# New transfer allowances and dates for the weight conversions that a planner makes ahead, and narrower ring dependencies

## The chip, the cores and the metric

The kernel runs on one core of one Trainium2 chip. The metric is the device time in microseconds (us) of one execution; less is better. The time of the kernel before is the median of three runs, and one further execution was taken by the hardware profiler.

## The reference, cut to what matters

An attention over 12 blocks of 128 tokens (two batches of 768, eight heads of 64, a local band of 96 tokens and 8 global ones) gives x of 1536 x 512. Two feed-forward layers follow, each 512 to 2048 to 512, all in float32 (the weights are float64 on the host):

```python
x = attention(q, k, v).reshape(1536, 512)
h = np.maximum(x @ moe_w_in, 0.0);  x = (h * h) @ moe_w_out
h = x @ moe2_w_in
g = np.where(h >= 1, h, np.where(h <= -1, 0.0, (h + 1) ** 2 / 4))
out = g @ moe2_w_out
```

## The kernel before

**Precision.** TensorE works on float32r, so each float32 operand is split into a high and a low part, and each product is three matmuls (high-high, low-high, high-low). ScalarE (ACT) makes the high part by a copy and VectorE (DVE) the low part by a subtraction (`copy` and `rest` of `Plan`).

**Weights.** A weight block c (128 hidden units of one layer, both matrices, 128x1024 float32) arrives as float64 words: two loads of 512 KB into a tile of the ring `raw` (two tiles). `float32` makes it float32 in a tile of the ring `whole` (three tiles in the middle of the kernel, two of them for good; the third lies in the tile m): for each half one ACTIVATE on ACT and three passes on DVE. `make` then splits it into one of nine slots from which TensorE reads it.

**Conversions made ahead.** The second layer runs through all its weights twice, and in pairs of blocks, with one product fewer per pair by the scheme of Strassen and Winograd, for which sums of the blocks are needed. So `prepare` converts each pair of blocks (c, c + 1) once, ahead, while the first layer still computes: four loads into `raw`, four ACTIVATEs, twelve DVE passes, two stores of 512 KB to DRAM (`kept`), four subtractions on GpSimd (POOL) or DVE into the tile `sumt`, and a store of that (`sums`). There are eight such preparations. Later `make_kept` loads `kept` and `sums` back into `whole` tiles and splits them into slots.

**Order.** Nothing is issued as it is written: every step is handed to a planner (`Plan.op`, `Plan.any_of`) with the engine or engines that may run it, a duration in ns, a due time and the keys it reads and writes. `emit` then runs a list schedule: an engine that is free takes, of the steps whose dependencies are met, the one that is due first. The order that comes out is the program order on each engine; on the chip the engines wait on semaphores only, so an engine whose next step is not ready stands, with all that is queued behind it. A step's `lag` is added to its end before its dependents may start: transfers have 1456 ns for 512 KB and, so far, `LAG` = 950 ns behind it. The keys also order the rings: a tile's next writer follows the readers of the one before, in the order in which the steps are handed in.

**Due times** count in events, one of which is a block of 128 hidden units against 512 tokens (24 matmuls of 512 columns). The first layer has 52 events (u = 0 to 51) with a total of 48 units; the 16 pair steps follow with 2.816 units each. `run` walks through the events and calls `prepare` for the next pair as soon as an event's due time reaches the preparation's date, which is `PREP + PREP_STEP * n`. With the dates before these are the events 25, 29, 32, 35, 38, 41, 44 and 47. The reloads of the first pair that need a slot of the first layer are handed in after events 45 and 46 (`make_after`).

**Places.** In the pair steps the accumulators p, u2, u3, u4 lie in a ring `u` of eight places of 384 columns in the tile pr; columns 0 to 2047 of pr hold the first layer's results of tokens 1024 to 1535 (keys `("save", 2, k)`) and columns 2048 to 3071 are `sumt`. `Plan.before` gives keys that the first writer of a place must also wait for. The lines that the change touches are the constants at L33, `float32` (L452), `prepare` (L484) and `instead` (L1292).

Of the kernel before, what the change touches and what calls it, by code (L numbers as in the profile page):

```python
# [29 lines left out]
G_LEAD = 2  # L30


PREP, PREP_STEP, LATE = 21, 3.1, 1  # L33
FIRST = -0.6, -0.4, 0.8

WARM, LAG = 10, 950
# [32 lines left out]
class Plan:  # L69
# [27 lines left out]
    def op(self, engine, ns, due, fn, reads=(), writes=(), lag=0, rows=P, tail=False, port=False):  # L97
        self.any_of([(engine, ns, fn, port)], due, reads, writes, lag, rows, tail=tail)
# [204 lines left out]
def ns_dve(n):  # L303
    return n / 0.96 + 70
# [11 lines left out]
class Ffn:  # L316
# [132 lines left out]
        plan.copy(w, d + 0.6, hi, f32[:, o:1024], keys, his, engines=WCOPY)  # L449
        plan.rest(w, d + 0.7, lo, f32[:, o:1024], hi, keys + his, los, engines=WREST)  # L450

    def float32(self, layer, c, due):  # L452

        nc, op = self.nc, self.plan.op
        kc, f32 = self.ring("whole")
        kr, raw = self.ring("raw")
        low, high, word = raw[:, :, 0], raw[:, :, 1], f32.bitcast(U32)
        for n in range(2):
            op("dma", 1456, due - W_LOAD + 0.1 * n, lambda n=n: nc.sync.dma_start(
                out=raw[:, 512 * n:512 * n + 512].rearrange("p f t -> p (f t)"), in_=self.w[layer][n][c],  # L460
            ), (), [(*kr, n)], lag=LAG)
        for n in range(2):
            h = slice(512 * n, 512 * n + 512)
            d = due - W_MAKE + 0.4 * n

            self.plan.scale(512, d, f32[:, h], high[:, h].bitcast(F32), 2.0 ** -112, [(*kr, n)], [(*kc, n)], engines=CONV)
            op("dve", ns_dve(256), d + 0.1, lambda h=h: nc.vector.tensor_scalar(  # L467
                out=word[:, h], in0=word[:, h], scalar1=3, scalar2=None, op0=ALU.logical_shift_left,
            ), (), [(*kc, n)], port=True)
            op("dve", ns_dve(512), d + 0.2, lambda h=h: nc.vector.scalar_tensor_tensor(  # L470
                out=word[:, h], in0=low[:, h], scalar=29, in1=word[:, h],
                op0=ALU.logical_shift_right, op1=ALU.bitwise_or,
            ), [(*kr, n)], [(*kc, n)], port=True)
            op("dve", ns_dve(512), d + 0.3, lambda h=h: nc.vector.scalar_tensor_tensor(  # L474
                out=word[:, h], in0=high[:, h], scalar=0x80000000, in1=word[:, h],
                op0=ALU.bitwise_and, op1=ALU.bitwise_or,
            ), [(*kr, n)], [(*kc, n)], port=True)
        return kc, f32
# [5 lines left out]
    def prepare(self, c, due):  # L484

        nc, op, plan = self.nc, self.plan.op, self.plan
        keys, tiles = [], []
        for n in range(2):
            kc, f32 = self.float32(1, c + n, due + LATE + n)
            ks = [(*kc, h) for h in range(2)]  # L490
            op("dma", 1456, due + LATE + 1 + n, lambda n=n, f32=f32: nc.sync.dma_start(out=self.kept[c + n], in_=f32),
               ks, [("kept", c + n)], lag=LAG)
            keys.append((*kc, 0))
            tiles.append(f32)
        kt, t = self.ring("sumt")
        SUMS = [("dve", ns_dve, nc.vector), ("pool", ns_pool, nc.gpsimd)]
        b11, b21, b12, b22 = (f32[:, 256 * n:256 * n + 256] for f32 in tiles for n in range(2))
        t1, t2, t3, t4 = (t[:, 256 * n:256 * n + 256] for n in range(4))
        for n, (out, in0, in1) in enumerate(((t1, b12, b11), (t3, b22, b12), (t2, b22, t1), (t4, b21, t2))):
            plan.any_of([(way, ns(256), lambda en=en, out=out, in0=in0, in1=in1: en.tensor_tensor(  # L500
                out=out, in0=in0, in1=in1, op=ALU.subtract), True) for way, ns, en in SUMS],
                due + LATE + 1 + 0.1 * n, keys, [kt])
        op("dma", 1456, due + LATE + 2, lambda: nc.sync.dma_start(out=self.kept_sums[c // 2], in_=t),
           [kt], [("sums", c)], lag=LAG)

    def parts(self, i, due, kc, f32):
        plan = self.plan
# [676 lines left out]
def kernel(  # L1184
# [38 lines left out]
    kept = [[dram.tile([P, 1024], F32, name=f"{name}{c}") for c in range(n)] for name, n in (("kept", 16), ("sums", 8))]  # L1223

    def tiles(s, f, plan):
# [18 lines left out]
        save = [pool.tile([P, 2048], F32, name=f"save{i}") for i in range(2)]  # L1244
# [47 lines left out]
        def instead():  # L1292

            b = f.plan.before
            for i in range(8):
                b["u", i] = [("save", 2, k) for k in range(4)] + [("sumt", 0)]
            for i in range(4):
                for part in range(2):
                    b["gq", i, part] = [("g512", i, part)] if i < 2 else [
                        (a, N_SLOTS - 1, h) for a in ("hi", "lo") for h in range(2)]  # L1300
            for i in range(2):
                b["rq", i] = [("r512", i)]
                for part in range(2):
                    b["xs", 4 + i, part] = [("raw", i, h) for h in range(2)]
                    b["o", 1 + i, part] = [("save", 3, k) for k in range(4)]
# [127 lines left out]
```

## Time and profile before

| what | value |
|---|---|
| median of 3 runs | 625.58 us |
| the three runs | 621.22, 625.58, 628.64 us |
| profiled execution | 628.68 us, of which the span from first to last instruction is 626.7 us |
| granted TensorE clock, mean | 0.99 |
| busy share of PE, DVE, ACT, POOL | 97%, 78%, 56%, 9% |
| bytes moved | 78.71 MB, mean 126 GB/s |

The profiled execution is 0.5% above the median and as long as the longest of the three runs. A busy share is the part of the span in which the engine had an instruction running; the two us between time and span lie outside the instructions.

### The profile page before, as it was taken

The page shows a single profiled execution, that of the slowest core. Times are in us where ns is not written, and L with a number is a line of the kernel's source. Part 1 is how long each engine was busy: PE and PEld are TensorE (multiplying, and loading weights), DVE is VectorE, ACT ScalarE, POOL GpSimd, SP SyncE. Part 2 cuts the span into 40 slices and gives each one's busy share as a digit, 9 for nine tenths or more (in the row PEclk, how much of TensorE's full clock was granted, in tenths as well). Part 3 has the DMA queues.
Part 4 walks back from the last instruction along what each step waited for, and adds up shares of the span by engine and source line. Part 5 has one row for each costly group of instructions (what it writes and reads, how often), then busy time and mean ns, then how long its engine had stood idle before and what let it go on. Part 6 is the DMA issues. An engine that isn't in the chain of part 4 may idle for free. (4 is left out here: it accounts for less than half of the span.)

```text
span 626.7 us, 9687 instructions
## 1 busy us (share of the span) xinstructions
PE 605.8 (97%) x3439; PEld 516.5 (82%) x3439; DVE 486.4 (78%) x1056; ACT 348.6 (56%) x720; POOL 58.5 (9%) x86
## 2 busy tenths in 40 slices
PE   7999999999999999979999999999999999999995
PEld 4788987887888888758888878888899888899884
DVE  5899999985638997768438569999988678887862
ACT  3898776965547765445347455554544445454431
POOL 4122020120100202222200200000000000000000
PEclk8999999999999999989999999999999999999999
DMA  7445444440014776896610430222220032222002
GB/s 268 150 150 173 135 153 135 136 169 18 27 41 133 252 258 237 274 352 236 210 55 0 155 132 35 93 93 94 93 92 35 0 136 93 92 93 92 27 1 106
DMA packets 25689, 78.71 MB, mean 126 GB/s; under 512 B 3104, under 2 KB 3104, under 8 KB 25632
## 3 DMA queue, kind: packets, MB, share of 16 engines
q1 hardware_dynamic: 25344, 78.00, 36.0%
q8 instruction: 29, 0.48, 0.3%
q14 instruction: 28, 0.23, 0.1%
q10 hardware_dynamic: 288, 0.00, 0.0%
HBM read 62.26 MB, written 15.73 MB: 124 GB/s over the span
## 5 line engine op out<-in xcount | busy, mean ns | idle before, releaser
L137 DVE TENSOR_TENSOR g<-r,g 128x512 fp32r<-128x512 f32 (+2 forms) x74 | 47.8, 646 | 36.0 <-ACT g L126 35.1
L655 DVE TENSOR_TENSOR pr<-bank,pr 128x384 f32<-128x384 f32 x112 | 60.0, 553 | 18.6 <-PE bank L649 17.7
L547 ACT ACTIVATE r<-bank 128x512 f32<-128x512 f32 (+1 forms) x52 | 29.2, 562 | 53.4 <-PE bank L532 52.1
L126 ACT ACTIVATE g<-r 128x512 fp32r<-128x512 f32 (+2 forms) x74 | 42.7, 577 | 23.3 <-DVE r L564 14.3
L893 ACT ACTIVATE pr<-pr,mn 128x256 f32<-128x256 f32 (+1 forms) x96 | 45.9, 482 | 10.3 <-DVE mn L888 10.0
L150 ACT ACTIVATE whole<-raw 128x512 f32<-128x512 f32 x52 | 34.0, 670 | 24.4 <-DMA raw<-in_moe_w_in_dram 7.7
L560 ACT ACTIVATE r<-pr,small 128x384 f32<-128x384 f32 x43 | 26.3, 616 | 33.8 <-DVE pr L655 33.6
L154 POOL TENSOR_SCALAR pr<-pr,mn 128x256 f32<-128x256 f32 (+1 forms) x39 | 25.4, 661 | 129.9 <-DVE mn L900 52.8
L474 DVE SCALAR_TENSOR_TENSOR whole<-raw,whole 128x512 uint32<-128x512 uint32 x52 | 37.3, 724 | 0.3
L470 DVE SCALAR_TENSOR_TENSOR whole<-raw,whole 128x512 uint32<-128x512 uint32 x52 | 36.9, 720 | 0.5
L888 DVE CUSTOM_DVE_ANT_0 pr<-bank,m 128x256 f32<-128x256 f32 (+1 forms) x96 | 33.2, 394 | 5.0 <-PE bank L952 5.0
L865 PEld LDWEIGHTS bank<-nat,nat 64*128 64x128 f32 x352 | 24.4, 200 | 9.9 <-issue 3.0
L467 DVE TENSOR_SCALAR whole<-whole 128x512 uint32<-128x512 uint32 x52 | 24.0, 468 | 10.6 <-ACT whole L150 9.8
L865 PE MATMUL bank<-nat,nat 64*128 64x128 f32 x352 | 28.9, 299 | 3.3 <-DVE mn L888 2.4
L562 DVE SCALAR_TENSOR_TENSOR r<-r 128x384 f32<-128x384 f32 x43 | 23.8, 556 | 6.0 <-ACT r L560 5.3
L126 ACT ACTIVATE pr<-bank 128x512 f32<-128x512 f32 (+2 forms) x47 | 24.3, 523 | 5.8 <-PE bank L916 2.3
L560 ACT ACTIVATE nat<-pr,small 128x384 f32<-128x384 f32 x21 | 12.9, 617 | 24.3 <-DVE pr L655 24.3
L564 DVE TENSOR_TENSOR r<-pr,r 128x384 f32<-128x384 f32 x43 | 23.8, 557 | 1.2
L916 PE MATMUL bank<-ident,pr 128*128 128x128 f32 x176 | 24.3, 277 | 0.2 <-DVE pr L152 0.2
L952 PE MATMUL bank<-pr,nat 128*64 128x128 f32 x352 | 23.6, 277 | 0.2
L916 PEld LDWEIGHTS bank<-ident,pr 128*128 128x128 f32 x176 | 20.3, 142 | 3.6 <-issue 0.9
L952 PEld LDWEIGHTS bank<-pr,nat 128*64 128x64 f32 x352 | 19.4, 136 | 4.2 <-issue 2.0
(343 smaller groups left out, 1755.6 us busy)
## 6 DMA issues: line engine op xcount, KB each, us to landing
raw<-in_moe_w_in_dram SPq DMA_DIRECT2D x32, 512.0 KB, 4.1
raw<-in_moe_w_out_dram SPq DMA_DIRECT2D x32, 512.0 KB, 4.1
whole<-sums SPq DMA_DIRECT2D x14, 512.0 KB, 3.2
whole<-kept SPq DMA_DIRECT2D x13, 512.0 KB, 3.2
kept<-whole SPq DMA_DIRECT2D x12, 512.0 KB, 6.2
whole<-kept SPq DMA_DIRECT2D x13, 384.0 KB, 2.9
sums<-pr SPq DMA_DIRECT2D x8, 512.0 KB, 6.0
nat<-in_k_dram SPq DMA_DIRECT2D x12, 256.0 KB, 3.5
```

Of the source, the lines that this page charges most:

```text
L126: ("act", ns_act(n) - 30 * psum, lambda: nc.scalar.activation(out=at(out), in_=in_, func=ACTF.Copy), False),
L137: ways = [("dve", ns_dve(n), lambda: nc.vector.tensor_tensor(out=at(out), in0=in_, in1=at(hi).bitcast(F32), op=ALU.subtract), not psum)]
L150: ("act", ns_act(n) + (0 if isinstance(by, float) else 107), lambda: nc.scalar.activation(out=out, in_=in_, func=ACTF.Copy, scale=by), False),
L470: op("dve", ns_dve(512), d + 0.2, lambda h=h: nc.vector.scalar_tensor_tensor(out=word[:, h], in0=low[:, h], scalar=29, in1=word[:, h], op0 ...
L474: op("dve", ns_dve(512), d + 0.3, lambda h=h: nc.vector.scalar_tensor_tensor(out=word[:, h], in0=high[:, h], scalar=0x80000000, in1=word[: ...
L560: op("act", ns_act(N) + 64, due, lambda: nc.scalar.activation(out=r, in_=h, func=ACTF.Relu, bias=self.half, scale=0.5), keys, [kr])
L655: op("dve", ns_dve(W), start + step[name] + 0.2 - G_LEAD, lambda: nc.vector.tensor_tensor(out=to, in0=area[kb], in1=in1, op=ALU.add), [("b ...
L865: nc.tensor.matmul(**c)
L888: op("dve", ns_dve(w), due, lambda e=e: nc.vector.tensor_tensor_reduce(out=pr[:, e, :w], in0=self.banks[kbs[e % 2]][:, e // 2 * 256:e // 2 ...
L893: op("act", ns_act(w) + 200, due, lambda e=e: nc.scalar.activation(out=pr[:, e, :w], in_=pr[:, e, :w], func=ACTF.Exp, bias=mn[:, e:e + 1], ...
L916: self.nc.tensor.transpose(self.banks[kbs[m]][:, o:o + P], pr[:, 2 * m + e, c * P:(c + 1) * P], self.ident)
L952: nc.tensor.matmul(**c)
```

## The change

The constants that date the preparations are changed: the first at 20 units in place of 21, and one every 2.75 units in place of 3.1. With these the calls fall to the events 24, 27, 30, 33, 35, 38, 41 and 44. A new constant `SLOW` = 3500 ns takes the place of `LAG` = 950 ns behind the transfers of a preparation (its loads of raw words, its stores to `kept`, its store to `sums`), so the planner lets a dependent start 4956 ns after such a transfer starts, where it was 2406 ns (and the hand-over between engines on top in both). The loads of `make` and `make_kept` keep `LAG`. In `instead`, a place of the ring `u` no longer waits for all of `save` 2 and `sumt`: places 0 to 5 wait for `save` 2, places 5 to 7 for `sumt`, as the columns lie. No instruction is added or taken away.

```diff
-PREP, PREP_STEP, LATE = 21, 3.1, 1
+PREP, PREP_STEP, LATE = 20, 2.75, 1
+
+SLOW = 3500
...
-    def float32(self, layer, c, due):
+    def float32(self, layer, c, due, lag=LAG):
...
                 out=raw[:, 512 * n:512 * n + 512].rearrange("p f t -> p (f t)"), in_=self.w[layer][n][c],
-            ), (), [(*kr, n)], lag=LAG)
+            ), (), [(*kr, n)], lag=lag)
...
-            kc, f32 = self.float32(1, c + n, due + LATE + n)
+            kc, f32 = self.float32(1, c + n, due + LATE + n, SLOW)
             ks = [(*kc, h) for h in range(2)]
             op("dma", 1456, due + LATE + 1 + n, lambda n=n, f32=f32: nc.sync.dma_start(out=self.kept[c + n], in_=f32),
-               ks, [("kept", c + n)], lag=LAG)
+               ks, [("kept", c + n)], lag=SLOW)
...
         op("dma", 1456, due + LATE + 2, lambda: nc.sync.dma_start(out=self.kept_sums[c // 2], in_=t),
-           [kt], [("sums", c)], lag=LAG)
+           [kt], [("sums", c)], lag=SLOW)
...
             for i in range(8):
-                b["u", i] = [("save", 2, k) for k in range(4)] + [("sumt", 0)]
+                b["u", i] = [("save", 2, k) for k in range(4)] * (i < 6) + [("sumt", 0)] * (i > 4)
```

## Rows read from the trace of the kernel before

**Rows 1.** The page, part 1: busy us, share and instructions of each engine

```profile
PE 605.8 (97%) x3439; PEld 516.5 (82%) x3439; DVE 486.4 (78%) x1056; ACT 348.6 (56%) x720; POOL 58.5 (9%) x86
```

**Rows 2.** Waits of engine PE: line, releaser, us in total, times, longest

```profile
...
PE bank L532 <- ACT r L547: 4.5, 1, 4.5
...
PE bank L730 <- DVE g L137: 1.4, 1, 1.4
PE bank L649 <- ACT pr L126: 1.3, 1, 1.3
...
```

**Rows 3.** Windows: stretch, length, busy of each engine, clock, DMA share, GB/s

```profile
...
270.65:275.15 4.50, 0.00 (x1) 0.00 (x0) 3.05 (x6) 1.16 (x3) 2.47 (x3) 1.00 0.97 347
275.15:282.00 6.85, 6.85 (x23) 5.47 (x24) 4.97 (x9) 4.52 (x9) 0.80 (x2) 0.75 0.92 319
...
363.00:615.00 252.00, 252.00 (x1250) 226.38 (x1249) 209.17 (x370) 118.92 (x198) 0.00 (x0) 1.00 0.21 73
...
```

**Rows 4.** Timeline of ACT, 240 to 280: start, length, work, [idle before, releaser]

```profile
...
245.35 0.67 ACT L150 ACTIVATE whole<-raw 128x512 f32<-128x512 f32 x1 [4.35 <-DMA raw<-in_moe_w_out_dram]
...
257.33 1.23 ACT L150 ACTIVATE whole<-raw 128x512 f32<-128x512 f32 x2 [5.25 <-DMA kept<-whole]
...
269.11 1.23 ACT L150 ACTIVATE m<-raw 128x512 f32<-128x512 f32 x2 [4.77 <-DMA kept<-m]
273.95 0.66 ACT L150 ACTIVATE whole<-raw 128x512 f32<-128x512 f32 x1 [3.62 <-DMA raw<-in_moe_w_in_dram]
...
```

**Rows 5.** Timeline of all engines where PE stood still

```profile
...
262.61 0.74 PE L730 MATMUL bank<-g,slot4h 128*128 128x512 f32 x2 [1.45 <-DVE g L137]
...
275.15 0.50 PE L532 MATMUL bank<-x,slot6h 128*128 128x512 f32 x1 [4.50 <-ACT r L547]
...
361.31 1.06 ACT L126 ACTIVATE slot3h<-whole 128x1024 fp32r<-128x1024 f32 x1 [2.44 <-DMA whole<-sums]
362.28 0.47 ACT L126 ACTIVATE pr<-bank 128x384 f32<-128x384 f32 x1
...
362.80 0.44 PE L649 MATMUL bank<-xs,slot0h 128*128 128x384 f32 x1 [1.26 <-ACT pr L126]
...
```

**Rows 6.** DMA issues, whole span: count, KB each, median us to landing

```profile
raw<-in_moe_w_in_dram SPq DMA_DIRECT2D x32, 512.0 KB, 4.1
...
kept<-whole SPq DMA_DIRECT2D x12, 512.0 KB, 6.2
...
```

**Rows 7.** The same from 262 to 275 us alone

```profile
...
kept<-whole SPq DMA_DIRECT2D x2, 512.0 KB, 8.3
...
```

**Rows 8.** Line L491 (stores of kept), 340 to 356 us: landing times

```profile
DMA to landing us min/median/max: 2.6/3.0/3.4
```

**Rows 9.** Timeline of SP's queue: stores of the sums, last step of each preparation

```profile
...
264.93 0.32 SPq L503 DMA_DIRECT2D sums<-pr  x1
...
276.06 0.33 SPq L503 DMA_DIRECT2D sums<-pr  x1
...
311.69 0.42 SPq L503 DMA_DIRECT2D sums<-pr  x1
...
355.47 0.43 SPq L503 DMA_DIRECT2D sums<-pr  x1
```

**Rows 10.** Windows of 10 us, columns as in the other windows

```profile
...
210.00:220.00 10.00, 10.00 (x46) 8.29 (x45) 9.62 (x16) 7.70 (x13) 1.45 (x2) 1.00 0.86 296
...
310.00:320.00 10.00, 10.00 (x46) 8.28 (x45) 0.82 (x2) 3.73 (x6) 0.00 (x0) 1.00 0.47 155
...
```

**Rows 11.** The page, part 5: ACT's and DVE's passes of one conversion

```profile
L150 ACT ACTIVATE whole<-raw 128x512 f32<-128x512 f32 x52 | 34.0, 670 | 24.4 <-DMA raw<-in_moe_w_in_dram 7.7
...
L474 DVE SCALAR_TENSOR_TENSOR whole<-raw,whole 128x512 uint32<-128x512 uint32 x52 | 37.3, 724 | 0.3
L470 DVE SCALAR_TENSOR_TENSOR whole<-raw,whole 128x512 uint32<-128x512 uint32 x52 | 36.9, 720 | 0.5
...
L467 DVE TENSOR_SCALAR whole<-whole 128x512 uint32<-128x512 uint32 x52 | 24.0, 468 | 10.6 <-ACT whole L150 9.8
```

## The prediction

> **What bounds the kernel.** I read the page's first part before anything else: PE is busy 605.8 of 626.7 us [rows 1], so the sum of the matmuls sets the time, and nothing that another engine does counts unless PE stands. The list of PE's waits tells where it stands. It has ten entries, of which seven, 6.3 us together, lie in the first 60 us, long before any step that the change dates. The other three are all that PE loses after that [rows 2]. From 363 to 615 us, the pair steps, PE is busy without a gap [rows 3]. So the change can only work between about 200 and 363 us, where the preparations run, and what it can win there is those three stops.
>
> The timeline says what they are [rows 5]. At 262.61 PE had stood 1.45 us for the low part of g on DVE; at 275.15 it had stood 4.50 us for a bank that ACT had not emptied; at 362.80 it had stood 1.26 us for ACT's copy of the first pair product. Behind each stands ACT in its own order of work, waiting for a transfer. Before the first, ACT waited 5.25 us at 257.33 for a store of `kept` that still read the `whole` tile that the next conversion was to fill; before the second, 4.77 us at 269.11 for another such store, and then 3.62 us at 273.95 for raw words [rows 4]; before the third, 2.44 us at 361.31 for a reload of sums, with the copy queued behind it [rows 5]. The same view has a wait of 4.35 us at 245.35 that cost PE nothing [rows 4]. So PE bears somewhat over 4 us of a late ACT, and pays from there on.
>
> The 4.50 us have a second price. In the 6.85 us after them the granted clock was 0.75 of full speed [rows 3], that is part at 2.4 and part at 1.2 GHz: a quarter of 6.85 us, 1.71 us, is lost. Together the stops cost 1.45 + 4.50 + 1.71 + 1.26 = 8.92 us of the profiled execution.
>
> Why ACT stood is an error of the planner. It placed the dependents of a transfer 1456 + 950 = 2406 ns after its start. Stores of `kept` took 6.2 us in the median and loads of raw words 4.1 [rows 6], and around the two large stops the stores took 8.3 [rows 7], while the DMA engines were 97% busy at 347 GB/s [rows 3].
>
> **The change part by part.** *The allowance of 3500 ns.* It changes no instruction, only which one ACT and DVE take next and when a tile's next use is planned. A dependent is now placed 4956 ns after the transfer's start. That is above the raw loads' 4.1 us and 1.24 us short of the stores' 6.2. An ACT that arrives 1.24 us early is far inside the 4 us that PE bears. But at 8.3 us it would be 3.34 us early, and two such waits in a row would pass the mark again. So it matters whether the transfers stay as crowded.
>
> I think that they don't. A preparation moves seven transfers of 512 KB, 3.67 MB. The last stores of the fourth and the fifth lie 276.06 - 264.93 = 11.13 us apart [rows 9], which is 330 GB/s, the rate at which the DMA engines were full. The planner packed them so closely because it thought the tiles free 2.55 us too early. Each conversion now holds its raw tile 2.55 us longer in the plan. With two such tiles that is 1.28 us per conversion, 2.55 us per preparation: about 13.7 us for one, my estimate from these rows, or 268 GB/s, three quarters of what ran at 97%. Stores then come nearer to the 2.6 to 3.4 us of a quiet stretch [rows 8] than to 8.3. I take nothing for the stops at 262 and 275 us and the clock after them, a gain of 1.45 + 4.50 + 1.71 = 7.66 us; the other end, if crowding stays, is no gain.
>
> *The dates.* A full event has 24 matmuls, and 46 matmuls fill 10 us [rows 10], so a unit is about 5.2 us. The first preparation is asked for 5.2 us earlier, and the step falls from 16.2 to 14.3 us. That calls the eighth at event 44 in place of 47. This is more than a date. Before, two reloads for the first pair had been handed in after events 45 and 46, ahead of it; they held both `whole` tiles until slots of the first layer came free. So the seventh preparation's sums were stored at 311.69 and the eighth's at 355.47, 43.8 us apart [rows 9]. Now it stands ahead of the reloads. Counting 13.7 us each from the fourth (264.93, less the 5.2 us of the earlier date) the eighth ends near 315 us. What moves is all of it: four loads and three stores on SP's queue, four ACTIVATEs of 670 ns (2.7 us), twelve DVE passes, 4 x (724 + 720 + 468) ns = 7.6 us [rows 11], and four subtractions on POOL. They enter a stretch in which DVE worked 0.82 us of 10 and ACT 3.73 [rows 10], so I cost them at nothing there; if that cover is gone, they cost no more than the 1.26 us that they cost at their old place. They leave the 15 us before the first pair, where they delayed the slot copies and reloads that ACT stood for at 361.31. On SP's queue the eighth is moved past the first reloads, which then go out some 20 us later; they are needed shortly before 362.80 [rows 5], which leaves over 20 us.
>
> On the other side the second and third preparations enter a stretch in which DVE was 96% busy, 210 to 220 us [rows 10]. The 7.6 us of a preparation don't fit into such a stretch. The bounds are nothing, because steps for PE are due earlier and go first, and 1.45 us, the nearest row in which a late low part of g stopped PE [rows 5]. I take nothing, for DVE at 96% let PE run through [rows 10], and keep 1.45 for the range.
>
> *The ring `u`.* The first write of place 0, the copy at 362.28 [rows 5], had to follow the last store of sums in the plan, issued at 355.47 [rows 9]. Without that key it may come earlier; with the eighth preparation gone by 315 us the key would not bind either. Together the two edits are worth between 0 and the 1.26 us of that stop. I take 1.26, since what ACT waited for there goes away with the eighth preparation. Places 6 and 7 belong to the second pair and meet nothing. No wait is added on the chip by any of this: the semaphores follow the tiles, and these stay.
>
> **The sum.** 628.68 - 8.92 = 619.76 us if every stop goes. A new order rarely closes without a small gap; I leave half of the smallest stop, 0.65 us, and forecast 620.4 us. The median of 625.58 lies 3.1 us below the profiled execution and the shortest run, 621.22, only 1.5 us above the floor, so I take the stops to differ from run to run with the landing times, and the gain against the median is 5.2 us, 0.8%.
>
> **The rivals.** *The transfers stay crowded, so the change doesn't do what it says.* If the planner fills the freed time with reloads and the loads of `make`, stores take 8.3 us again and the stops stay: 625.6 us, the median. For it: 4956 ns is well under 8.3. Against it: the longer hold of the tiles itself thins the traffic. A milder form keeps one stop of 4.50 with its 1.71 us of clock and loses the rest, 619.76 + 6.21 = 626.0 in the worst run, some 623 in the median.
>
> *The allowance is too long.* Where traffic is thin, stores land in 2.6 to 3.4 us [rows 8], and a plan that waits 4.96 us holds tiles for nothing. Then the preparations stretch, the eighth slips back into the pair's start, and the 1.26 us stay: 620.4 + 1.26 = 621.7 us. The section "Anatomy of one DMA" of the Trainium skill's page "DMA: Bandwidth & Descriptors" speaks for this: it gives a fixed part of about 2.0 us and the bytes at 436 GB/s, an estimate of 3.2 us for 512 KB, and by it the allowance would be 1.8 us too long. This case's trace agrees in the quiet stretch alone; the median of 6.2 us [rows 6] does not. I give it a chance of 0.15.
>
> *Slower: the new order stops PE elsewhere with the clock.* The place is 200 to 260 us, where DVE and ACT are most loaded and two more conversions are pressed in. One stop long enough to lower the clock costs 4.50 + 1.71 = 6.21 us. One leaves the kernel where it was; it is slower from the second on, 619.76 + 12.42 = 632.2 us, 1.1% above the median. Against it: the first stop of PE in that part of the kernel is that at 262.61 us [rows 5]; DVE at 96% did not stop it [rows 10].
>
> **How the numbers follow.** Forecast, all or nearly all stops gone (619 to 621.5): 0.52. Allowance too long (621.7): 0.15. Still crowded, in part or wholly (623 to 626): 0.22. Slower (632): 0.07; what I can't name on either side: 0.04. The range reaches from 618.4, the floor less the 1.4 us by which a run without the first stop could still differ, to 626.0, and takes in the 1.45 us of DVE and the milder crowding. About 1% is what a measurement of this kernel can tell from no change. Faster by over 1% means under 619.3, half a us below the floor: I give 0.32, for a median of before that comes out above 625.58 makes it so. Within 1%: 0.59. Slower by over 1%: 0.09.
>
> **What would show it.** Right: no wait of PE between 200 and 363 us in the list of waits, a clock of 1.00 there, ACT's waits for `kept` stores under 4 us, sums stored some 13 to 14 us apart with the last near 315, and DMA shares under 0.9 in each 10 us. Wrong: stores that land at 8 us as before, a stop of PE before 260 us with DVE's g behind it, or a preparation that still ends after 340 us. A time well below 619 would mean that the first 60 us differ from run to run as well, which the rows of one execution can't exclude.

## The result, and the profile after

The changed kernel takes 618.99 us (median of 13 runs, 618.29 to 619.77) where the kernel before, in as many runs, took 625.54 (621.22 to 628.64). The ratio is 0.9903, with a 95% interval of 0.9886 to 0.9920. The profiled execution took 618.29 us with a span of 616.3, against 628.68 and 626.7 before. The runs also lie closer together: 1.5 us from the shortest to the longest, where it was 7.4.

The page's first part: PE is busy for 2.4 us less in all, in a span that is 10.4 us shorter [rows 1].

```profile
PE 603.4 (98%) x3439; PEld 516.0 (84%) x3439; DVE 483.0 (78%) x1053; ACT 348.6 (57%) x720; POOL 61.1 (10%) x89
```

All of PE's waits in the kernel after (line, releaser, us in total, times, longest us). The three entries that answered for the stops [rows 2] are gone, and the six that are left lie in the first 60 us. The changed kernel is two lines longer ahead of these, so L532 of before is L534 here.

```profile
PE bank L867 <- DMA nat<-in_q_dram: 1.5, 1, 1.5
PE bank L1334 <- DVE warm L1332: 1.2, 1, 1.2
PE bank L1339 <- ACT r L549: 0.9, 2, 0.5
PE bank L732 <- ACT g L128: 0.5, 1, 0.5
PE bank L534 <- DVE x L139: 0.2, 1, 0.2
PE bank L918 <- DVE pr L154: 0.2, 1, 0.2
```

The windows of the kernel after, columns as in [rows 3]. PE is busy all the time at full clock, while DVE is busy for 99 to 100% of two stretches and the DMA engines are as full as before: a share of 1.01 by this view, at 369 GB/s.

```profile
240.00:250.00 10.00, 10.00 (x46) 8.27 (x45) 9.93 (x14) 6.12 (x11) 4.23 (x4) 1.00 0.91 285
...
260.00:270.00 10.00, 10.00 (x46) 8.28 (x45) 8.83 (x15) 5.47 (x10) 3.75 (x4) 1.00 1.01 369
270.00:280.00 10.00, 10.00 (x46) 8.29 (x45) 9.98 (x18) 7.92 (x15) 3.23 (x3) 1.00 0.85 296
```

ACT's timeline of the kernel after, which answers to [rows 4]. A conversion still waits for raw words, 1.58 us at most here, and the emptying of the bank (L549) stands behind it only shortly. From 264 us on that emptying has caught up and waits for PE itself, 1.63 and 1.88 us: ACT is early where it was late.

```profile
257.10 0.67 ACT L152 ACTIVATE whole<-raw 128x512 f32<-128x512 f32 x1 [1.58 <-DMA raw<-in_moe_w_in_dram]
...
264.47 0.60 ACT L549 ACTIVATE r<-bank 128x512 f32<-128x512 f32 x1 [1.63 <-PE bank L534]
...
269.91 0.60 ACT L549 ACTIVATE r<-bank 128x512 f32<-128x512 f32 x1 [1.88 <-PE bank L534]
```

The transfers did not land sooner. The landing times of the stores of `kept` between 190 and 365 us, first before, then after:

```profile
DMA to landing us min/median/max: 2.6/6.2/8.3
```

```profile
DMA to landing us min/median/max: 2.6/6.2/8.4
```

The loads of raw words took rather longer in this stretch: 5.0 us in the median, 4.3 before.

A measure for the stops follows from two landmarks on PE between which its order is the same in every kernel here: the last products of the attention and the first product of the pair steps. Before:

```profile
173.90 1.97 PE L952 MATMUL bank<-pr,nat 128*64 128x128 f32 x32
...
355.79 0.33 PE L649 MATMUL bank<-x,slot7h 128*128 128x384 f32 x1
```

After:

```profile
172.48 1.97 PE L954 MATMUL bank<-pr,nat 128*64 128x128 f32 x32
...
345.87 0.33 PE L651 MATMUL bank<-x,slot7h 128*128 128x384 f32 x1
```

Start to start it was 181.89 us and is 173.39, so 8.50 us went there: the first two stops and the low clock after them. The third stop lies behind the second landmark, from which to the last matmul (619.30 and 607.85 us) it was 263.51 and is 261.98, another 1.53. The first landmark came 1.42 us earlier, before any step that the change dates, and the tail after the last matmul was 1.05 us longer (7.40 and 8.45). The four make the span's 10.4 us: 8.50 + 1.53 + 1.42 - 1.05.

### The profile page after: what moved, and what is told of

Read it like the earlier page. It is cut to its first block, busy times and chain, and to the rows that moved or that the text cites. A ratio compares the mean times of both kernels' runs of the same rounds, so it can differ in the third digit from the quotient of the medians.

```text
span 616.3 us, 9688 instructions
## 1 busy us (share of the span) xinstructions
PE 603.4 (98%) x3439; PEld 516.0 (84%) x3439; DVE 483.0 (78%) x1053; ACT 348.6 (57%) x720; POOL 61.1 (10%) x89
## 4 chain that ended last, share of the span: by engine, by line
PE 93%; DMA 2%; DVE 2%; ACT 1%; issue 0%; SPq 0%; ACTq 0%; DVEq 0%
PE bank L534 22%; PE bank L732 21%; PE bank L701 21%; PE bank L651 19%; PE bank L867 4%; PE bank L954 3%; PE bank L918 3%; DMA nat<-in_q_dram 1%; DMA out_dram<-save 1%; DMA raw<-in_moe_w_in_dram 1%; DVE pr L890 1%; PE bank L1339 0%; DVE whole L472 0%; ACT pr L895 0%; ACT pr L128 0%
## 5 line engine op out<-in xcount | busy, mean ns | idle before, releaser
L139 DVE TENSOR_TENSOR g<-r,g 128x512 fp32r<-128x512 f32 (+2 forms) x74 | 49.1, 663 | 36.0 <-ACT g L128 35.0
L549 ACT ACTIVATE r<-bank 128x512 f32<-128x512 f32 (+1 forms) x52 | 29.2, 562 | 63.8 <-PE bank L534 62.5
L476 DVE SCALAR_TENSOR_TENSOR whole<-raw,whole 128x512 uint32<-128x512 uint32 x52 | 36.7, 711 | 0.4
L472 DVE SCALAR_TENSOR_TENSOR whole<-raw,whole 128x512 uint32<-128x512 uint32 x52 | 35.4, 691 | 0.3
```

Of the source, the lines that this page charges most:

```text
L139: ways = [("dve", ns_dve(n), lambda: nc.vector.tensor_tensor(out=at(out), in0=in_, in1=at(hi).bitcast(F32), op=ALU.subtract), not psum)]
```

## The experiments

The theory after the result: the allowance works through the order of ACT's steps, in that the emptying of PE's banks is no longer queued behind conversions whose data are not there. The rivals: the dates do it; the allowance does it by thinning the transfers, as the prediction had it; any other order would do. Each ratio is against runs of the kernel before on the same chip. The ratios and their intervals are not the quotients of the two medians beside them and differ from those by up to 0.003.

The table has one profile of each kernel: the landmarks, their distance, what it is over 173.39, the way from the second landmark to the last matmul ("to the end"), and how late ACT was to empty a bank. That is the time from the end of the twelve products of a block on PE to the start of the step that empties their bank (L547, in other kernels L549 or L551), the longest between 200 and 330 us:

```
kernel        first    second   distance   over   to the end   latest emptying
before        173.90   355.79   181.89     8.50   263.51       6.58
after         172.48   345.87   173.39     0      261.98       0.20
ring_only     173.02   353.83   180.81     7.42   261.97       5.21
dates_only    172.73   352.73   180.00     6.61   261.97       4.78
slow_only     172.61   346.00   173.39     0      264.07       0.08
slow_dates    172.83   346.22   173.39     0      261.97       0.12
loads_slow    172.65   346.04   173.39     0      261.98       0.12
stores_slow   172.56   348.16   175.60     2.21   261.96       3.68
slow_1500     173.69   347.08   173.39     0      261.94       1.23
slow_2200     172.71   346.09   173.38     0      261.97       2.40
slow_6000     172.89   346.28   173.39     0      262.23       0.07
before_twice  172.82   350.83   178.01     4.62   262.85       5.19
after_twice   172.85   346.24   173.39     0      261.96       0.80
lag_all       174.13   347.52   173.39     0      261.97       0.56
```

In the nine kernels at the floor ACT was never more than 2.40 us late in that stretch; in each of the five others it was 3.68 to 6.58 us late at least once.

**The parts, one at a time.** *ring_only* is the kernel before with the new dependencies of the ring `u` alone:

```diff
-                b["u", i] = [("save", 2, k) for k in range(4)] + [("sumt", 0)]
+                b["u", i] = [("save", 2, k) for k in range(4)] * (i < 6) + [("sumt", 0)] * (i > 4)
```

> Only the ring dependencies are changed; dates 21 and 3.1 and the allowance of 950 ns stay. Theory of the allowance (the stops come from dependents placed too early behind transfers): the two stops near 262 and 275 us stay; at most the 1.26 us stop at the pairs' start goes, so 624.3 to 625.5 us, ratio 0.998 to 1.000. Theory of the dates (the stops come from when the preparations are asked for): the same. If the ring carried the gain: 619 to 621 us.

Measured: 624.79 us against 626.21, ratio 0.9986 (0.9963 to 1.0008). The two large stops stay, as 3.1 us for ACT and 1.4 for DVE; the third, the copy of the first pair product, is no longer in PE's list, and the way from the second landmark to the end is at its least. A gain of its size can't be told from none in the time.

*dates_only* has the new dates alone:

```diff
-PREP, PREP_STEP, LATE = 21, 3.1, 1
+PREP, PREP_STEP, LATE = 20, 2.75, 1
```

> Only the dates 20 and 2.75; the allowance stays at 950 ns, the ring dependencies as before. Theory of the allowance: preparations are packed at least as closely, stores of kept still land 6 to 8 us after issue, and ACT still waits for them for 4 to 5 us at a time, so PE keeps one or two stops of 1.5 to 4.5 us and the clock falls once: 623 to 627 us. Theory of the dates: the eighth preparation leaves the pairs' start, the stops go, 619 to 621 us.

Measured: 624.29 us against 626.21, ratio 0.9978 (0.9960 to 0.9995). The eighth preparation does move, its sums being stored at 308.23 us, and still the landmarks lie 6.61 us too far apart. ACT's waits for transfers between 190 and 365 us, and under them PE's waits after 60 us that they lead to, in this run:

```profile
ACT whole L150 <- DMA raw<-in_moe_w_out_dram: 11.7, 7, 3.1
ACT whole L150 <- DMA raw<-in_moe_w_in_dram: 8.1, 4, 3.3
ACT whole L150 <- DMA kept<-whole: 6.3, 3, 4.1
...
```

```profile
PE bank L532 <- ACT r L547: 2.1, 1, 2.1
PE bank L730 <- ACT g L126: 1.7, 3, 0.7
...
PE bank L730 <- DVE g L137: 0.8, 1, 0.8
```

(One of the three waits of the second line, 0.5 us long, belongs to the first 60 us, as in the kernel after.) The stops are more and shorter than before, but the dates alone do not take them away. So another order as such is not enough: ring_only and dates_only each have one.

*slow_only* has the allowance alone (`SLOW` as in the change, the dates 21 and 3.1, the ring as before):

```diff
+SLOW = 3500
...
-            kc, f32 = self.float32(1, c + n, due + LATE + n)
+            kc, f32 = self.float32(1, c + n, due + LATE + n, SLOW)
...
-               ks, [("kept", c + n)], lag=LAG)
+               ks, [("kept", c + n)], lag=SLOW)
...
-           [kt], [("sums", c)], lag=LAG)
+           [kt], [("sums", c)], lag=SLOW)
```

> Only the allowance of 3500 ns; dates and ring dependencies as before. Theory of the allowance: no stop between 200 and 300 us, ACT's waits for kept stores under 2 us each; the eighth preparation still runs at 340 to 355 us and leaves the stop of 1.26 us there: 619.5 to 621 us. Theory of the dates: the stops stay, 623 to 627 us.

Measured: 619.77 us against 626.21, ratio 0.9905 (0.9878 to 0.9932), and the distance of the landmarks at its floor. ACT's waits for transfers are 1.7 us in total. What the dates would have saved shows behind the second landmark: the eighth preparation's sums are stored at 345.28 us, and in the pair steps, at 397 and 431 us, the low parts of two slots come late:

```profile
PE bank L651 <- DVE slot5l L139: 0.8, 1, 0.8
...
PE bank L651 <- DVE slot1l L139: 0.6, 1, 0.6
```

*slow_dates* is the change without its ring part:

```diff
-                b["u", i] = [("save", 2, k) for k in range(4)] * (i < 6) + [("sumt", 0)] * (i > 4)
+                b["u", i] = [("save", 2, k) for k in range(4)] + [("sumt", 0)]
```

> The allowance and the dates, but the ring dependencies as before. Both theories: 618.5 to 619.5 us, as with all three parts, since the last sums are stored some 45 us before the first pair writes place 0. If the ring carried part of the gain: 620 to 621 us with a stop of 1 to 2 us at the pairs' start.

Measured: 619.00 us, ratio 0.9894 (0.9867 to 0.9921). It is as fast as the whole change, so the ring part is worth nothing that shows beside the others. It differs from slow_only by the dates alone: 0.77 us between the medians, and 2.10 us behind the second landmark in the two profiles. The intervals are wider than 0.77 us, but they hold the spread of the kernel before as well; set side by side, five of the six times of slow_dates lie below all six of slow_only.

**Which transfers, and how much.** *loads_slow* and *stores_slow* each have one half of the allowance, with the new dates and ring:

```diff
-               ks, [("kept", c + n)], lag=SLOW)
+               ks, [("kept", c + n)], lag=LAG)
...
-           [kt], [("sums", c)], lag=SLOW)
+           [kt], [("sums", c)], lag=LAG)
```

> All of the change but for the stores: the loads of raw words of a preparation have 3500 ns, the stores of kept and of the sums 950 ns. If the stores' allowance is what counts (the longest waits of ACT before the stops were for stores of kept): waits for kept stores of 3 to 5 us return, PE stops for 1.5 to 6 us, 620.5 to 625 us. If the loads' is what counts, because it alone spaces the conversions: 619 us, as with all parts.

```diff
-            kc, f32 = self.float32(1, c + n, due + LATE + n, SLOW)
+            kc, f32 = self.float32(1, c + n, due + LATE + n)
```

> All of the change but for the loads: the stores of kept and of the sums have 3500 ns, the loads of raw words 950 ns. If the stores' allowance is what counts: ACT waits for raw words for 1 to 3 us at a time, which PE bears, 619 to 620.5 us. If the loads' is what counts: 622 to 625 us.

Measured: 618.26 us, ratio 0.9887 (0.9852 to 0.9923), and 620.20 us, ratio 0.9914 (0.9887 to 0.9941), both against 625.31. The loads alone do all of it, though the longest waits before the stops were for stores. The stores alone do most. Their run is instructive, for ACT waits about as long for transfers as in the kernel before, 26 us in all against 27:

```profile
ACT whole L152 <- DMA raw<-in_moe_w_out_dram: 12.9, 8, 3.2
ACT m L152 <- DMA kept<-m: 4.0, 1, 4.0
ACT m L152 <- DMA raw<-in_moe_w_in_dram: 3.7, 1, 3.7
ACT whole L152 <- DMA raw<-in_moe_w_in_dram: 3.7, 2, 2.9
ACT whole L152 <- DMA kept<-whole: 1.7, 1, 1.7
...
```

and yet the landmarks are only 2.21 us over the floor. So the total of ACT's waits doesn't tell what PE loses.

*slow_2200*, *slow_6000* and *slow_1500* have all three parts with another allowance:

```diff
-SLOW = 3500
+SLOW = 2200
```

> All three parts with an allowance of 2200 ns in place of 3500, so dependents stand 3656 ns after a transfer's start, below the 4.1 us median of the loads and half of what crowded stores took. If it is the order of ACT's work that counts and PE bears 4 us of a late ACT: waits of 2 to 4 us return, 619 to 621 us. If the full allowance is needed: 622 to 625 us.

> All three parts with 6000 ns, 7456 ns from a transfer's start to its dependent, as long as the crowded stores took. If an allowance that is too long holds the tiles for nothing: preparations over 14 us apart, the last after 330 us, a stop of PE at the pairs' start, 620.5 to 623 us. If only the order of ACT's work counts: no wait of ACT for a transfer, 618.5 to 619.5 us.

> All three parts with 1500 ns in place of 3500: 2956 ns from start to dependent, against 2406 before and 3656 in the run with 2200. Looks for where the gain sets in. If any longer allowance does: 619 to 620 us. If it sets in between 1500 and 2200: 622 to 625 us, with waits of ACT of 3 to 4 us and stops of PE.

Measured: with 1500 ns 617.76 us against 623.98, ratio 0.9869 (0.9804 to 0.9933); with 2200 ns 618.51 against 625.31, 0.9894 (0.9855 to 0.9934); with 6000 ns 618.93 against 625.31, 0.9892 (0.9857 to 0.9927). From 1500 to 6000 ns there is one level, and each has the same distance of the landmarks. 950 ns with the same dates is dates_only (the ring part taken as worth nothing here too). So the gain sets in between 950 and 1500 ns, far below what the transfers take, which between 230 and 270 us is 6.8 and 7.0 us in slow_1500 and 6.8 and 6.5 in dates_only (medians for stores of `kept`, from `whole` and from the tile m). An allowance of 6000 ns costs nothing either: the sums are stored some 13 us apart, the last at 318.36 us.

**Later landings.** *before_twice* and *after_twice* store each `kept` block twice, the second time to a DRAM tile that nobody reads, before and after the change:

```diff
+            op("dma", 1456, due + LATE + 1 + n, lambda n=n, f32=f32: nc.sync.dma_start(out=self.spare[c + n], in_=f32),
+               ks, [("spare", c + n)], lag=SLOW)
```

(with `LAG` in before_twice).

> The kernel before, with each store of kept made twice (the second copy goes to a DRAM tile that nobody reads): one MB more per preparation, and a whole tile is free only when both have landed. The result is the reference's. If the stops come from dependents that stand in ACT's order before their transfer has landed: later landings lengthen ACT's waits, PE's stops after 200 us grow from 7 to 10 to 20 us, 630 to 638 us. If landing times don't matter: 625 to 627 us.

> The changed kernel, with each store of kept made twice in the same way, both with 3500 ns, so that the planner knows of the second. If the allowance works by the order of ACT's work and not by thinner traffic: stores land after 7 to 9 us, and PE still runs through, 618.5 to 620 us. If it works only while transfers land soon: stops return, 622 to 628 us.

Measured: after_twice takes 618.32 us against 623.98, ratio 0.9882 (0.9818 to 0.9946), with landings of 8.1 and 7.4 us (the two stores of a `whole` tile, medians, 230 to 270 us), the DMA engines 100% busy from 270 to 300 us, and no stop. This is what the theory of the order asks for. before_twice is a miss for both theories: 621.29 us, ratio 0.9949 (0.9915 to 0.9983), faster than before with half a MB more per block to store. Nor did it do what it was made for: its landings were not later, 5.9 and 6.8 us for the two stores of a `whole` tile where the kernel before took 7.9. The second store goes through the planner too, with 1456 ns of its transfer engine, so a tile's next use is planned later; that this works like a longer allowance is my reading and was not tested by itself. Its ACT timeline has the longest wait for a transfer of all runs:

```profile
297.80 0.67 ACT L150 ACTIVATE whole<-raw 128x512 f32<-128x512 f32 x1 [6.10 <-DMA spare<-whole]
298.37 0.58 ACT L549 ACTIVATE r<-bank 128x512 f32<-128x512 f32 x1
```

PE did not stop for it. Its timeline in the same run: the products that L549 is to empty ended with the matmul at 295.62 us, so for most of the 6.10 us ACT had nothing to empty, and it was 2.4 us late.

```profile
295.62 0.39 PE L534 MATMUL bank<-x,slot2h 128*128 128x512 f32 x1
...
298.57 0.39 PE L534 MATMUL bank<-x,slot1h 128*128 128x512 f32 x1
```

The kernel before at its large stop, timeline of PE and of ACT:

```profile
267.55 0.39 PE L532 MATMUL bank<-x,slot6h 128*128 128x512 f32 x1
...
270.26 0.39 PE L730 MATMUL bank<-g,slot5h 128*128 128x512 f32 x1
```

```profile
274.52 0.58 ACT L547 ACTIVATE r<-bank 128x512 f32<-128x512 f32 x1
```

The products ended at 267.94 us, the emptying began at 274.52, 6.6 us late; PE had the y products to do until 270.65 and then stood. So a wait of ACT counts from the moment at which PE's products are ready, not from its own start.

How much PE covers depends on the place. Before the change the block that PE wants next at 270.65 us has the same weights as the one that ended at 267.94 (slot6h in both; the start at 275.15 us is in [rows 5]): both are block 15, for two groups of tokens. By the kernel's `[0, 1, 6, 7][c % 4]` they also have the same bank, so PE stands until that bank is empty. It covered 2.1 us there (6.58 late, a stop of 4.50), and as much in ring_only (5.21 late, a stop of 3.1). Elsewhere the next block has another bank. In before_twice an emptying was 5.2 us late at such a place, and the one at the place with one bank was on time, having waited for PE:

```profile
248.20 0.58 ACT L549 ACTIVATE r<-bank 128x512 f32<-128x512 f32 x1
...
268.01 0.60 ACT L549 ACTIVATE r<-bank 128x512 f32<-128x512 f32 x1 [1.43 <-PE bank L534]
```

PE's timeline around the first of the two: its products ended at 243.02 us, it began the next block at 247.07, ahead of the emptying, and stood 0.22 us for the high part of g:

```profile
242.63 0.39 PE L534 MATMUL bank<-x,slot2h 128*128 128x512 f32 x1
...
247.07 0.39 PE L534 MATMUL bank<-x,slot3h 128*128 128x512 f32 x1
...
250.16 0.50 PE L732 MATMUL bank<-g,slot2h 128*128 128x512 f32 x1 [0.22 <-ACT g L126]
```

No single wait of PE in before_twice is longer than 0.6 us after the first 60 us. So it did not lose what the kernel before lost at the shared bank, the 4.50 us and the clock behind them: its late emptyings fall where PE has another bank. The 2.4 us at 298 us, which is such a place, are no limit for the place at 275.

The first stop of the kernel before, 1.45 us, is not one of a bank. PE waited for the low part of g on DVE, and that stood in DVE's order behind the six passes of the conversion for which ACT had waited 5.25 us:

```profile
258.03 0.99 DVE L467 TENSOR_SCALAR whole<-whole 128x512 uint32<-128x512 uint32 x2 [4.30 <-ACT whole L150]
...
261.34 1.21 DVE L137 TENSOR_TENSOR g<-r,g 128x512 fp32r<-128x512 f32 x1
```

It is the same fault, a step that PE needs queued behind a conversion whose data are late, on the next engine.

**Elsewhere.** *lag_all* gives 2200 ns to all other transfers as well:

```diff
-WARM, LAG = 10, 950
+WARM, LAG = 10, 2200
```

> The changed kernel, with 2200 ns in place of 950 for all other transfers too: loads of q, k and v, the loads of the first layer's conversions and the reloads of kept and sums. The order of the attention changes with it. PE has no stop after 60 us in the changed kernel, so nothing is to be won there; if the first 60 us have stops by transfers that land late, 617 to 618.5 us; if not, 618.5 to 620 us, and more if the other order of the attention fits worse.

Measured: 618.64 us against 623.98, ratio 0.9882 (0.9818 to 0.9947): nothing beyond the change. No run here is faster than the changed kernel by more than the intervals.

## Why the prediction was right, and where its working was not

- **The bound and the size.** The three stops and the clock behind them were all that PE lost after the first landmark, and nearly all that was won between the two profiled executions. They were put at 8.92 us and measured at 8.50 + 1.53 = 10.03; the waits and the mean clock miss about 1 us of it. Between the medians the gain is 6.55 us (5.2 was forecast); it is smaller there because the profiled execution of before was as long as the longest of its runs. The floor of 619.76 us for the profiled execution was therefore high: the runs of the change have a median of 618.99, and the 0.65 us that the forecast left for a small new gap did not come up. The forecast of 620.4 was 1.4 us too long.
- **The step that failed: thinner traffic.** The prediction took nothing for the stops because each preparation would take 13.7 us, so that 268 GB/s would let the stores land soon. The sums after the change are stored at these times on SP's queue (four of the eight):

```profile
248.15 0.33 SPq L505 DMA_DIRECT2D sums<-pr  x1
...
258.03 0.33 SPq L505 DMA_DIRECT2D sums<-pr  x1
...
268.72 0.33 SPq L505 DMA_DIRECT2D sums<-pr  x1
...
307.03 0.42 SPq L505 DMA_DIRECT2D sums<-pr  x1
```

  The first three are 9.9 and 10.7 us apart, closer than the 11.13 of before [rows 9]; the later ones are 10.6 to 14.0 apart. From 230 to 270 us the core moved 337 GB/s, before 273, DMA shares reached 1.01, and the median landing time stayed at 6.2 us. Of the prediction's own signs of being right the spacing and the shares failed, and stores that take 8 us, a sign of being wrong, were seen (8.4 at most). So, against what the prediction held, it did not matter whether the transfers stay as crowded; its rival "the transfers stay crowded" came true in its condition and not in its time. By the prediction's own reckoning stores of 8.3 us leave ACT 3.34 us early, and two such waits in a row bring the stops back; that the forecast came out all the same is luck in this step. Nor was it the stores, whose landing times it weighed most: the loads' allowance alone does all. In place of it the runs show the order: with 1500 ns or more ACT's order empties PE's banks in time (1.23 us late at most with 1500), and with 950 ns it does not (4.78), at the same dates and with landing times of the same size.
- **The 4 us that PE bears** was read from the length of ACT's waits. It should be read from the end of PE's products to the start of the step that empties them: the wait of 4.35 us at 245.35 that cost nothing left the emptying only 1.84 us late (245.93 us). And it is not one number: about 2.1 us where two blocks in a row share a bank; elsewhere an emptying 5.2 us late cost a stop of 0.22 us (before_twice, 248 us).
- **The dates** did what was said of the eighth preparation (forecast near 315 us, last sums at 307.03), and ACT and DVE took it there without a stop. Their worth, put within the 1.26 us of the third stop, measured 0.77 us between the medians of slow_only and slow_dates. The DVE crowding between 200 and 260 us cost nothing, as taken.
- **The ring** was put between 0 and 1.26 us together with the dates. Alone it takes the third stop away in its profile; with the dates there is nothing left for it.
- **The allowance too long** (0.15) is refuted up to 6000 ns. The section "Anatomy of one DMA — SWDGE (gpsimd) path" of the Trainium skill's page "DMA: Bandwidth & Descriptors" has its figures for transfers that GpSimd issues; the estimate of 3.2 us that they make for 512 KB lies above the shortest landing of a store here (2.6 us, issued on SP's queue) and far below the median of 6.2.
- **Slower** did not happen in any run with one part or with all: no ratio here is above 1.

What stays open is why the planner's order turns between 950 and 1500 ns and not at another value; its decisions were not followed step by step. No run gave the two blocks that share a bank a bank each, so whether that alone would have taken the large stop away is open too.

## What to carry to other kernels

Where engines run in program order, a plan need not know the true landing time of a transfer; it must not put a step that the bounding engine waits for behind one that may still wait. Look at the step that frees the bounding engine and measure how late it starts after its input was ready: that, not the sum of an engine's waits, is what a stop is made of. Then ask what the bounding engine can do meanwhile, above all whether its next work needs the very buffer that is waited for. When the executions of one kernel differ by 7 us and those of another by 1.5, stops that hang on landing times are a thing to look for; that they made the spread here is likely and was not measured.

## What the runs showed that I had not expected

Denser traffic with a better order was faster: 337 GB/s against 273 from 230 to 270 us, and PE without a stop. A kernel that stores half a MB more per block than the kernel before (before_twice) took 0.5% less. And the first landmark, 170 us in, ahead of all that the change dates, moved by 1.4 us between profiled executions of before and after, about as much as the spread of the changed kernel's runs.
